# An attention and mixture-of-experts kernel: two more chunks through crossbar transposes, and another order of loads

## Chip, cores and metric

The kernel runs on one core of one Trainium2 chip. The metric is device time in microseconds (us) of one execution, the median of several executions. The profile comes from one execution of its own, and its span is the time from the first to the last instruction that it shows.

## What is computed

Two stages follow each other. The first is a linear attention with decay, for 4 batches, 8 heads, 768 time steps and 48 numbers per head. The second sends every one of the 3072 resulting rows (384 numbers each) through four experts, all of them, and adds their outputs with weights.

```python
# B, H, S, D = 4, 8, 768, 48
for t in range(S):
    cur = np.einsum('bhd,bhe->bhde', u[None] * kt, vt)
    y[:, :, t] = np.einsum('bhd,bhde->bhe', rt, state + cur)
    state = w[None, :, :, None] * state + np.einsum('bhd,bhe->bhde', kt, vt)
# x: (3072, 384), rows in the order batch, time
p = domain_probs / (domain_probs.sum(-1, keepdims=True) + 1e-09)
for e in range(4):
    h = np.maximum(x @ w1[e], 0.0)       # w1[e]: 384 x 1024
    out += p[:, e:e + 1] * (h @ w2[e])   # w2[e]: 1024 x 384
```

## The kernel before

**Tiling.** Time is cut into chunks of 128 steps. Chunk ci belongs to batch ci % 4 and time block ci // 4, so there are 24 chunks, and four chunks in a row (one of each batch) make a "sub-block" sc, six in all. All matrix work is in bf16, loads and accumulations in f32.

**Attention of a chunk.** R and K (r and k of the chunk) are scaled with powers of the decay on VectorE (DVE) or GpSimd (POOL), written into the buffer RK (line 332). RK is transposed for each pair of heads, which gives RKT. TensorE (PE) multiplies the two halves of RKT to scores (At, line 436), DVE multiplies those with a triangular mask (AtM, line 445), and PE multiplies by V and by the running state S (Y, lines 467 and 474). POOL forms r*k*u (ruk, lines 345 and 353), DVE sums it per head (dcoef, line 366), and POOL multiplies it by V (dv, line 371). Ysb is Y plus dv (line 483). The state is renewed through PE (line 515), DVE (line 530) and POOL (line 535). Ysb is transposed into xTe, the input of the experts.

**Two ways to transpose.** With `ci < DMAT` a chunk is transposed on PE against an identity matrix (RK at line 394, Ysb at line 500), and ScalarE (ACT) or DVE copies the result out of PSUM into RKT and xTe. With `ci >= DMAT` SP issues a crossbar DMA that transposes from SBUF to SBUF (RKT at line 378, xTe at line 490), and no engine copies. The same number decides over the scores: from DMAT on, an even chunk and the odd one after it are multiplied together in one job of PE ("paired"), which begins when both have their RKT. The odd chunk's scores then take a "tr" and an "mm" bank of PSUM in place of two "At" banks:

```python
dmat = ci >= DMAT
...
paired = ci >= DMAT
tags = ("tr", "mm") if paired and ci % 2 else ("At", "At")
```

**Experts.** A slot is one expert e on one sub-block sc. Its first layer (l1) fills hT_ps in eight groups: chunk by chunk, with 128 columns a matmul (line 596), in the slots (0,0), (0,1) and (1,1), and for the four chunks together, with 512 columns (line 602), in all others. ACT applies the ReLU (lines 611 and 613). The second layer (l2, line 632) is eight matmuls of 384 columns for each chunk, then DVE or ACT adds it into oacc with the weight of the expert (lines 640 and 642). The order of the slots is (0,0), (1,0), (0,1), (1,1), (2,0), (2,1), (3,0), (3,1), and then the four experts of each further sub-block.

**Weights.** w1 and w2 of an expert come in three pieces each (576, 576 and 384 KB) into eight staging tiles (wst) and are cast to bf16 into w_sb on ACT, DVE or POOL (lines 72, 74 and 76). A group of l1 needs only the pieces that hold its columns.

**What sets the order.** SP issues all loads, all crossbar transposes and all stores, in one queue. Its loads come in a written order, the string `ORDER` (line 219): K, R and V with a chunk number, "w1e0.1" for piece 1 of w1 of expert 0, "p" for the probabilities. From chunk 14 on the rest follows chunk by chunk. All other orders come from a planner that runs as the program is built (from line 675): every piece of work is a job with the engines it may run on, what it needs, a rank and the buffers it takes and gives back. The planner plays them through and writes down which engine takes which job when. The instructions are then issued per engine in that order, each engine strictly in line. So an instruction that has to wait holds up all that was planned behind it on its engine or queue. What an instruction really needs is enforced by semaphores whether or not the job lists it. In the first 20 us, where PE has too little work, matmuls on a constant (line 173) are put into its gaps.

Of the kernel before, what the change touches and what calls it, by code (L numbers as in the profile page):

```python
# [19 lines left out]
def kernel(  # L20
# [109 lines left out]

    WARM, NSPIN = 6.6, 6
    TAIL = {"T": 0.27, "V": 0.17, "A": 0.20, "P": 0.17, "S": 0.0}
    DMAT = 8
    BACKLOG = 6.0
    HURRY = 30.0
    PAD_PE, PAD = 1.0, 0.4
# [13 lines left out]
    def job(name, on, run, needs=(), rank=0.0, takes=(), drops=(), moves=None,  # L150
            behind=()):
        j = Job()
        j.behind = behind
        j.name, j.on, j.run, j.needs, j.rank = name, on, run, list(needs), rank
        j.takes, j.drops, j.moves = takes, drops, moves
        for k in drops:
            tokens[k] = tokens.get(k, 0) + 1
        j.pad = 0.0
        ci = name[1] if isinstance(name, tuple) and name[0] in ATT else -1
        if ci >= SUB:  # L160

            j.pad = PAD_PE if "T" in on else PAD
        j.no = len(jobs)
        assert name not in jobs
        jobs[name] = j
# [49 lines left out]
    def load_p():  # L215
        load_job("prow", (0.36, 2), lambda: nc.sync.dma_start(
            prow, moe_domain_probs.rearrange("(n p) e -> n p e", p=C)))

    ORDER = ("K1 R1 K0 R0 V0 R2 K2 V1 w1e0.1 w1e0.2 K3 w1e0.0 R3 V2 w2e0.0 V3 w2e0.1 w2e0.2 p w1e1.2 "
             "w1e1.1 R4 w1e1.0 K5 K4 w2e1.0 w2e1.2 w2e1.1 R5 V4 w1e2.2 w1e2.1 K6 w1e2.0 V5 K7 w2e2.2 "  # L220
             "w2e2.1 w2e2.0 R6 V6 K8 V7 R7 w1e3.2 w1e3.0 K9 w1e3.1 w2e3.0 V9 R9 R8 V8 V11 V10 R11 "
             "K10 R10 K12 K11 w2e3.1 V12 w2e3.2 R13 R12 K13 V13 " +
             " ".join(f"c{i}" for i in range(14, TOTC))).split()
    for what in ORDER:
        if what == "p":
# [87 lines left out]
    def attention(ci):  # L313
        b, c = ci % B, ci // B
        RK = RKB[ci % NRK]
        dmat = ci >= DMAT

        rk = float(ci)
        on_pe = -20.0 + 0.01 * ci
        pre = [("S", ci - NRK), ("T", ci - NRK, 1)] if ci >= NRK else []  # L320
        if ci >= 2 * SUB:

            e_g, sc_g, one = SLOTS[ci - LEAD - (ci % 2 if ci >= DMAT else 0)]
            pre.append(("l1", e_g, sc_g, 0, 0))
# [44 lines left out]
        def dv():  # L369
            tl["dv", ci] = work.tile([128, H, D], F32, tag="dv", bufs=3, name="dv")  # L370
            nc.gpsimd.tensor_mul(tl["dv", ci], tl["Vt", ci],  # L371
                                 tl["dcoef", ci].to_broadcast((128, H, D)))
        job(("dv", ci), {"P": 0.82}, dv, [("dcoef", ci)], rk - 0.4, (("dv", ci),), (("inp", ci),))

        if dmat:
            def tr():
# [47 lines left out]

        paired = ci >= DMAT
        tags = ("tr", "mm") if paired and ci % 2 else ("At", "At")
# [118 lines left out]
    for ci in range(TOTC):  # L545
        attention(ci)
# [309 lines left out]
```

## Time and profile before

| | |
|---|---|
| Median of 4 runs | 297.04 us (296.8 to 299.72) |
| Profiled execution | 297.05 us, its span 295.3 us |
| PE busy | 286.5 us, 97% of the span |
| DVE busy | 153.5 us, 52% |
| ACT busy | 153.0 us, 52% |
| POOL busy | 103.5 us, 35% |
| Granted clock of TensorE | 1.0 throughout |
| Moved by DMA | 37.66 MB, DMA engines full for about the first 90 us |

A busy share says how long an engine had an instruction in it. For PE the ends of the matmuls are modelled and neighbours overlap, so a single duration (326 ns for 384 columns) is longer than the time that it adds. What it adds is read from one start to the next. The chain of waits, followed back from the last instruction, is on PE for 81% of the span and on transfers for 7%. Here is its summary in the page, share of the span by engine and line:

```profile
PE 81%; DMA 7%; SPq 4%; POOL 2%; DVE 2%; issue 2%; ACT 2%; POOLq 0%; DVEq 0%
PE out_ps L632 37%; PE hT_ps L602 34%; DMA wst<-in_moe_w_dram 7%; PE hT_ps L596 4%; SPq L191 3%; PE At_ps L436 1%; PE Y_ps L474 1%; PE St_ps L515 1%; PE Y_ps L467 1%; POOL S L535 1%; ACT w_sb L72 1%; SPq L202 1%; POOL ruk L353 1%; DVE RK L332 1%; POOL dv L371 1%
```

### The profile page before, as it was taken

To read this page: it belongs to the slowest core of one execution; us is meant where nothing else is said; L and a number is where in the kernel's file an instruction comes from. 1 tells how busy PE (TensorE), PEld (TensorE's weight loads), DVE (VectorE), ACT (ScalarE), POOL (GpSimd) and SP (SyncE) were. 2 spreads that over 40 slices of the span, in tenths; PEclk is the share of its full clock that TensorE was granted. 3 is DMA by queue.
4 is the path that set the end of the run, shared out by engine and by line. 5 is a ranking of instruction groups with operands and counts; after the bars stand their busy time and mean duration, and the time that the engine had idled before them with its cause. 6 is when DMAs were issued, how large, how long until landed. Compare 5 with 4: busy or idle time off the path is not lost.

```text
span 295.3 us, 5781 instructions
## 1 busy us (share of the span) xinstructions
PE 286.5 (97%) x2264; PEld 169.3 (57%) x2293; DVE 153.5 (52%) x298; ACT 153.0 (52%) x251; POOL 103.5 (35%) x138
## 2 busy tenths in 40 slices
PE   8989999999989999999999999999999999999995
PEld 2777556868745555555555555555555555555553
DVE  6966879588494857526537436545404322101223
ACT  3685958754484444464543564443464444565440
POOL 3783243838949556443522443501000000000000
PEclk9999999999999999999999999999999999999999
DMA  7999999899999397392093393130340100200003
GB/s 147 270 259 338 258 275 300 192 300 188 242 179 178 72 201 193 95 196 47 16 175 82 109 175 61 28 71 29 97 83 0 27 2 27 80 2 0 0 2 107
DMA packets 111199, 37.66 MB, mean 128 GB/s; under 512 B 99242, under 2 KB 111148, under 8 KB 111172
## 3 DMA queue, kind: packets, MB, share of 16 engines
q1 hardware_dynamic: 111156, 37.29, 52.8%
q8 instruction: 18, 0.29, 0.4%
q14 instruction: 9, 0.07, 0.1%
q10 hardware_dynamic: 16, 0.00, 0.0%
HBM read 26.79 MB, written 4.72 MB: 107 GB/s over the span
## 4 chain that ended last, share of the span: by engine, by line
PE 81%; DMA 7%; SPq 4%; POOL 2%; DVE 2%; issue 2%; ACT 2%; POOLq 0%; DVEq 0%
PE out_ps L632 37%; PE hT_ps L602 34%; DMA wst<-in_moe_w_dram 7%; PE hT_ps L596 4%; SPq L191 3%; PE At_ps L436 1%; PE Y_ps L474 1%; PE St_ps L515 1%; PE Y_ps L467 1%; POOL S L535 1%; ACT w_sb L72 1%; SPq L202 1%; POOL ruk L353 1%; DVE RK L332 1%; POOL dv L371 1%
## 5 line engine op out<-in xcount | busy, mean ns | idle before, releaser
L613 ACT ACTIVATE hTs<-hT_ps 128x512 bf16<-128x512 f32 x168 | 99.5, 597 | 94.0 <-PE hT_ps L602 89.0
L632 PE MATMUL out_ps<-w_sb,hTs 128*128 128x384 bf16 x760 | 138.8, 326 | 0.3 <-DVE oacc L642 0.2
L602 PE MATMUL hT_ps<-xTe,w_sb 128*128 128x512 bf16 x475 | 122.0, 379 | 2.2 <-ACT hTs L613 0.8
L632 PEld LDWEIGHTS <-hTs 128*128 128x128 bf16 x760 | 72.6, 98 | 53.2 <-issue 0.5
L642 DVE SCALAR_TENSOR_TENSOR oacc<-out_ps,p_nat,oacc 128x384 f32<-128x384 f32 x71 | 43.7, 616 | 89.4 <-PE out_ps L632 89.2
L602 PEld LDWEIGHTS <-w_sb 128*128 128x128 bf16 x504 | 47.0, 98 | 47.6 <-issue 1.0
L445 DVE TENSOR_TENSOR AtM<-At_ps,mask 128x512 bf16<-128x512 f32 x48 | 30.8, 682 | 16.3 <-PE At_ps L436 16.3
L345 POOL TENSOR_TENSOR ruk<-Rt,Kt 128x384 f32<-128x384 f32 x24 | 24.9, 1040 | 40.9 <-DMA Kt<-in_k_dram 28.6
L371 POOL TENSOR_TENSOR dv<-Vt,dcoef 128x384 f32<-128x384 f32 x24 | 20.1, 840 | 44.1 <-DVE Ysb L483 30.0
L353 POOL TENSOR_TENSOR ruk<-ruk,U_sd 128x384 f32<-128x384 f32 x23 | 23.4, 1019 | 0.9
L640 ACT ACTIVATE oacc<-out_ps,p_nat 128x384 f32<-128x384 f32 x24 | 13.9, 582 | 14.3 <-PE out_ps L632 14.1
L72 ACT CAST w_sb<-wst 128x1152 bf16<-128x1152 f32 (+1 forms) x13 | 13.7, 1053 | 13.8 <-DMA wst<-in_moe_w_dram 13.5
L535 POOL TENSOR_TENSOR S<-Tn,wC 64x192 bf16<-64x192 f32 x32 | 18.6, 580 | 5.4 <-DVE Tn L530 4.0
L366 DVE TENSOR_REDUCE dcoef<-ruk 128x8 f32<-128x384 f32 x24 | 13.1, 547 | 13.9 <-POOL ruk L353 13.8
L596 PE MATMUL hT_ps<-xTe,w_sb 128*128 128x128 bf16 x288 | 18.6, 219 | 1.0 <-ACT w_sb L72 0.9
L596 PEld LDWEIGHTS <-w_sb 128*128 128x128 bf16 x288 | 16.8, 98 | 2.2 <-ACT w_sb L72 1.2
L611 ACT ACTIVATE hTs<-hT_ps 128x512 bf16<-128x512 f32 x24 | 14.3, 597 | 6.2 <-PE hT_ps L596 5.0
L332 DVE TENSOR_TENSOR RK<-Kt,W_sd 128x384 bf16<-128x384 f32 x20 | 15.8, 796 | 1.0 <-DMA Kt<-in_k_dram 0.9
L483 DVE TENSOR_TENSOR Ysb<-Y_ps,dv 128x384 bf16<-128x384 f32 x24 | 13.2, 552 | 5.0 <-PE Y_ps L474 4.9
L76 POOL CAST Vb<-Vt 128x384 bf16<-128x384 f32 x20 | 10.9, 546 | 9.0 <-PE St_ps L515 3.7
L530 DVE TENSOR_TENSOR Tn<-S,St_ps 64x192 f32<-64x192 bf16 x32 | 11.2, 349 | 2.7 <-PE St_ps L515 2.0
L332 DVE TENSOR_TENSOR RK<-Rt,W_sd 128x384 bf16<-128x384 f32 x20 | 12.0, 599 | 1.1 <-DMA Rt<-in_r_dram 0.9
(67 smaller groups left out, 134.4 us busy)
## 6 DMA issues: line engine op xcount, KB each, us to landing
wst<-in_moe_w_dram SPq DMA_DIRECT2D x16, 576.0 KB, 6.4
Kt<-in_k_dram SPq DMA_DIRECT2D x24, 192.0 KB, 3.9
Rt<-in_r_dram SPq DMA_DIRECT2D x24, 192.0 KB, 3.7
Vt<-in_v_dram SPq DMA_DIRECT2D x24, 192.0 KB, 3.6
out_dram<-oacc SPq DMA_DIRECT2D x23, 192.0 KB, 1.9
wst<-in_moe_w_dram SPq DMA_DIRECT2D x8, 384.0 KB, 6.5
RKT<-RK SPq DMA_TRANSPOSE x16, 3.2
xTe<-Ysb SPq DMA_TRANSPOSE x16, 2.4
```

The lines of the kernel that those rows point to most:

```text
L72: nc.scalar.copy(o, i)
L332: eng.tensor_mul(RK[:, i, :, 0:D], tl[("Kt", "Rt")[1 - i], ci], tl["W", i] if ci < SUB and i not in on_pool else W_sd[i])
L345: nc.gpsimd.tensor_mul(tl["ruk", ci], tl["Rt", ci], tl["Kt", ci])
L353: nc.gpsimd.tensor_mul(tl["ruk", ci], tl["ruk", ci], U_sd)
L371: nc.gpsimd.tensor_mul(tl["dv", ci], tl["Vt", ci], tl["dcoef", ci].to_broadcast((128, H, D)))
L445: nc.vector.tensor_mul(tl["AtM", ci][:, j], tl["At", ci, j], mask[:, None, :].to_broadcast((128, NP, C)))
L535: nc.gpsimd.tensor_mul(S_new[pr, :, cl], tl["Tn", ci][pr], wC[pr, :, None].to_broadcast((P2, NP, D)))
L596: nc.tensor.matmul(ps[:, i, :], w1_sb[:, e, db, (fb + i) * 128:(fb + i + 1) * 128], xTe[:, db, s0, :], start=(i == 0 and db == 0), stop=(i ...
L602: nc.tensor.matmul(ps[:, 0:n, :].rearrange("p a b -> p (a b)"), w1_sb[:, e, db, fb * 128:(fb + 1) * 128], xTe[:, db, s0:s0 + n, :].rearran ...
L613: nc.scalar.activation(hTs[:, fb, s0:s0 + n, :], ps[:, 0:n, :], AF.Relu)
L632: nc.tensor.matmul(ps, tl["hTs", e, sc][:, fb, s, :], w2_sb[:, e, fb, :], start=(fb == 0), stop=(fb == NFB - 1))
L642: nc.vector.scalar_tensor_tensor(tl["oacc", ci], in0=tl["o", e, ci], scalar=pe, in1=tl["oacc", ci], op0=ALU.mult, op1=ALU.add)
```

## The change

Three edits. DMAT goes from 8 to 6, so chunks 6 and 7 are transposed by DMAs, and their scores are computed as a pair. The order of the loads up to chunk 13 is another one, with the same 67 loads. And the job that forms dv lists the load of V among the things it needs, beside dcoef; the instruction itself is the same.

```diff
-    DMAT = 8
+    DMAT = 6
...
-    ORDER = ("K1 R1 K0 R0 V0 R2 K2 V1 w1e0.1 w1e0.2 K3 w1e0.0 R3 V2 w2e0.0 V3 w2e0.1 w2e0.2 p w1e1.2 "
-             "w1e1.1 R4 w1e1.0 K5 K4 w2e1.0 w2e1.2 w2e1.1 R5 V4 w1e2.2 w1e2.1 K6 w1e2.0 V5 K7 w2e2.2 "
-             "w2e2.1 w2e2.0 R6 V6 K8 V7 R7 w1e3.2 w1e3.0 K9 w1e3.1 w2e3.0 V9 R9 R8 V8 V11 V10 R11 "
-             "K10 R10 K12 K11 w2e3.1 V12 w2e3.2 R13 R12 K13 V13 " +
+    ORDER = ("V0 R1 K0 R0 K1 R2 w1e0.1 K2 V1 w1e0.2 w1e0.0 R3 V2 K3 w2e0.0 V3 w2e0.1 p w2e0.2 w1e1.2 "
+             "K5 R4 w1e1.0 K4 w1e1.1 w2e1.0 R5 w2e1.1 w2e1.2 w1e2.1 w1e2.0 V4 w1e2.2 V5 K7 K6 R7 R6 "
+             "w2e2.2 V7 V6 R8 w2e2.0 R9 w2e2.1 V8 w1e3.1 K8 K9 w1e3.2 w1e3.0 V9 K10 K11 R10 R11 V10 "
+             "R12 w2e3.1 V11 R13 K13 w2e3.0 V12 K12 w2e3.2 V13 " +
              " ".join(f"c{i}" for i in range(14, TOTC))).split()
...
-        job(("dv", ci), {"P": 0.82}, dv, [("dcoef", ci)], rk - 0.4, (("dv", ci),), (("inp", ci),))
+        job(("dv", ci), {"P": 0.82}, dv, [("dcoef", ci), ("Vt", ci)], rk - 0.4, (("dv", ci),), (("inp", ci),))
```

## The prediction

> **What bounds the kernel now.** I read the busy times by stretch first, then TensorE's waits, its timeline where the moved chunks lie, and last the transfers. In the rows below the columns are the stretch, its length, busy time of the engines with instruction counts, granted clock, busy share of the DMA engines, GB/s.
>
> ```profile
> 0.00:20.00 20.00, 17.09 (x196) 11.46 (x197) 14.62 (x42) 11.89 (x21) 12.39 (x22) 1.00 0.89 216
> 20.00:30.00 10.00, 9.88 (x139) 8.01 (x137) 6.39 (x17) 6.04 (x11) 4.81 (x5) 1.00 1.11 328
> ...
> 60.00:70.00 10.00, 9.87 (x111) 6.68 (x109) 9.93 (x19) 4.37 (x4) 4.78 (x7) 1.00 1.03 262
> 70.00:80.00 10.00, 10.00 (x137) 7.99 (x134) 4.58 (x10) 5.94 (x10) 9.37 (x14) 1.00 1.03 205
> 80.00:90.00 10.00, 9.14 (x72) 4.93 (x72) 8.32 (x16) 7.55 (x12) 6.29 (x8) 1.00 0.98 211
> 90.00:100.00 10.00, 9.72 (x75) 5.29 (x75) 6.86 (x13) 2.99 (x5) 7.79 (x11) 1.00 0.72 138
> ```
>
> TensorE (first busy column) is full from 20 us on: the stretches between 20 and 250 us together leave 2.55 us idle, 1.14 of it between 80 and 100. At the same time the DMA engines are full until 90 us. So two things run at their limit side by side, and PE sets the end as long as the loads keep it fed. Before 20 us much of PE's busy time is filler (matmuls of line 173); real work follows without a gap from 18.82 us, when the first expert's weights are there. TensorE's own waits confirm it:
>
> ```profile
> PE hT_ps L596 <- ACT w_sb L72: 0.9, 2, 0.5
> PE hT_ps L602 <- ACT hTs L613: 0.8, 1, 0.8
> ```
>
> They are us in total, times, longest. Hardly anything is there to recover by waiting less.
>
> **What the Trainium skill says.** "Trainium Kernel Development and Optimization", Performance Expectations, calls matmul busy time a poor measure, since matmuls overlap. I therefore checked spacing: eight matmuls of 384 columns take 1.30 us start to start in the chain, again and again up to 290 us, and other work leaves the gaps. PE is really full. "VectorE: DVE Perf Modes", The three transpose paths, prices a 128x128 transpose at 390 ns on TensorE and 1309 ns by crossbar DMA. The trace disagrees for runs of them: on PE eight take 0.45 us, 56 ns each; a DMA of eight tiles lands after 3.2 us, not 10.5. "Advanced Engine Details and Errata", X-Bar Transpose (TRN2), says such DMAs are as fast as regular ones; I use that below. "DMA: Bandwidth & Descriptors", Queues, rings and completion order, says that what SP issues shares one row of rings, consumed in order: a transpose stands behind the loads issued before it. The trace agrees: 4.7 us at most to landing, in the loaded stage, against 3.1 at least.
>
> **The change, part by part.**
>
> *1. Transposes and scores of chunks 6 and 7 (DMAT 8 to 6).* PE's timeline, columns start, duration, then what:
>
> ```profile
> 56.47 0.61 PE L394 MATMUL RKT_ps<-ident,RK 128*128 128x128 bf16 x8
> 56.92 1.46 PE L632 MATMUL out_ps<-w_sb,hTs 128*128 128x384 bf16 x8
> ...
> 60.28 0.40 PE L436 MATMUL At_ps<-RKT 64*128 64x128 bf16 x8
> 60.61 0.62 PE L394 MATMUL RKT_ps<-ident,RK 128*128 128x128 bf16 x8
> 61.07 2.76 PE L632 MATMUL out_ps<-w_sb,hTs 128*128 128x384 bf16 x16
> ...
> 72.13 0.33 PE L500 MATMUL xT_ps<-ident,Ysb 128*128 128x128 bf16 x3
> 72.30 1.46 PE L632 MATMUL out_ps<-w_sb,hTs 128*128 128x384 bf16 x8
> ...
> 77.68 0.62 PE L436 MATMUL At_ps<-RKT 64*128 64x128 bf16 x16
> 78.23 2.77 PE L632 MATMUL out_ps<-w_sb,hTs 128*128 128x384 bf16 x16
> ```
>
> Start to next start: each L394 group 0.45 and 0.46, each L500 group 0.17 (the other one is at 67.44, followed at 67.61). Scores alone cost 0.33 and 0.34 (60.28 and 64.33), a pair 0.55. PE sheds 0.45 + 0.46 + 2 x 0.17 + (0.67 - 0.55) = **1.37 us**, all in the full stage. ACT loses two copies of 1.01 us, DVE two of 0.36; neither is the bound, so I count nothing.
>
> In their place SP issues two transposes RKT<-RK and two xTe<-Ysb, about 1.24 and 1.18 us of SP each, in the stage where its queue carries all loads. The page's issues (KB each, median us to landing):
>
> ```profile
> wst<-in_moe_w_dram SPq DMA_DIRECT2D x16, 576.0 KB, 6.4
> ...
> RKT<-RK SPq DMA_TRANSPOSE x16, 3.2
> xTe<-Ysb SPq DMA_TRANSPOSE x16, 2.4
> ```
>
> What they take of the DMA engines has no row. From the stretches: 70 to 80 us, with two RKT transposes, moved 205 GB/s where 60 to 70, equally busy, moved 262; 10 us x 57/262 = 2.2 us, or 1.1 each. By the skill's "as fast as regular", estimated at 262 GB/s, RKT (256 KB) takes 1.0 and xTe (96 KB) 0.4. I take 2 x 1.1 + 2 x 0.4 = 3.0 us by which later loads slip; between 0 and 3.0 reaches the end, see 3. Chunk latency grows too: PE transpose plus copy was about 1.7 us (56.47 to 58.17), now 3.2 to 4.7; Xout 0.5 to 1 us, now 2.4 to 3.3. Chunk 6's scores also wait for chunk 7. Cover: R7 moves forward by 2304 KB in the order and R6 by 1344, some 9.8 and 5.7 us at 20.4 MB in 87 us (0.235 MB/us), far more than the added latency. Four masks of 0.65 us now come in one row on DVE, which is full from 60 to 70; the two pairs of scores hold one of four "mm" banks for about 2.6 us. I count 0, bound 0.5.
>
> *2. The start.* I added up the order. K0 and R0 keep their places, w1e0.1 lies 384 KB earlier, w1e0.0 192 KB earlier. The ACT row that opens PE's full stretch is
>
> ```profile
> 17.61 1.15 ACT L72 CAST w_sb<-wst 128x1152 bf16<-128x1152 f32 x1 [0.65 <-DMA wst<-in_moe_w_dram]
> ```
>
> 192 KB at 216 GB/s is 0.9 us. Chunk 1 has its xTe at 18.06 and chunk 2's V comes earlier too, so PE can fill up 0.9 us earlier. K3 comes 960 KB later, 4 us, but chunk 3's hidden layer was computed only at 28.4 us with its input there by 26. Yet w1e1.1 now comes 1152 KB later, about 33 us instead of 28.5, and ready after its cast at some 34.3. PE would by then have used up expert 0 and five of eight groups of expert 1. The lead survives in part: gain **0.4**, bounds 0 and 0.9.
>
> *3. The loads around 60 us.* w2e2.1 moves back 1728 KB. It was cast at about 52.2 to 52.9 and used from 61; 1728/235 = 7.4 us plus 2.2 for two RKT transposes ahead of it makes it ready at 62.5. What can PE do without it? From 36.6 us: second half of expert 1 (32 x 0.1625 = 5.2), first half of expert 2 (5.2), chunks 4 and 5 of experts 0 and 1 (4 x 2.65 = 10.6), their attention 3.0: until 60.6; scores, Y and state of chunks 6 and 7 (1.65): until 62.2 if their transposes land by 57. The hole is 0 to 2 us; I take **+0.6**. Later loads (w1e3 576 KB later, w2e3 576 KB) have cover: the first half of expert 2 on chunks 4 to 7 alone is 5.2 us, and the chunks they compete with come sooner. Of the 0.86 us idle at 80 to 90, which is ACT casting w2e3 pieces ahead of a ReLU, I take away 0.2; bounds -1.1 and +0.5.
>
> *4. dv needs Vt.* No instruction is added; the data dependence existed already. POOL waited 8.9 us for Vt in front of two dv (39.88 and 46.72), with the next chunk's ruk queued behind; now other POOL work can stand there. PE did not wait for it, so I count 0: POOL idles 65% of the span, and that is the cover. Bounds 0 and, if ruk in front makes a dv late by its 1.0 us, 0.5.
>
> Sum: -1.37 - 0.4 + 0.6 - 0.2 + 0 = **-1.4**, span 295.3 to 293.9. Profiled execution 297.05 = 295.3 + 1.75 around it, and the median of the runs 297.04 is the same. Forecast 295.6.
>
> **Rivals.** *A, nothing gained:* the loads are the clock of the stage to 90 us, and 3.0 us of added DMA time reaches PE in part or in full. With half of it, 297.0 - 1.37 + 1.5 = 297.2; in full, 298.7. I give 297.9. For it: DMA share 1.03 at 60 to 80. Against: PE idles only 0.13 us from 50 to 80, so some lead exists.
>
> *B, slower by a blocked queue:* SP issues in order. If it reaches a transpose before DVE has written RK or Ysb, every load behind it waits. The queue holds a lead of about 4 us (576 KB land after 6.4 us and need 2.2 themselves). SP waited 5.7 us for RK and 11.1 for Ysb at worst in the run before, harmless because the loads were already out. Such waits at 50 to 65 us cost 1.7 to 7 beyond the lead, and PE has no slack there: -1.4 + 5 = 300.6 (299 to 303). It decides from an SP wait of about 7 us, the lead plus 3. Against: R6, R7, K6, K7 stand together in the new order, so RK is early.
>
> *C, everything holds:* -1.37 - 0.9 - 1.1 = 293.7. That requires no hole at 34 or 62 us.
>
> That the edit doesn't do what it says is excluded: the choice is made by chunk number, with no data condition.
>
> **Numbers.** Forecast (294.1 to 297.0) 0.50, A 0.20, B 0.19, C 0.11. A measurement of this kernel tells about 1% from no change, that is 294.07 and 300.01. Faster is C with 0.11; slower is B with 0.19; the rest, forecast and A, is 0.70. The range 293.5 to 300.2 leaves out half of B and the edge of C, about 0.15.
>
> **What would show it.** Right: 48 transposing matmuls of L394 in place of 64, 18 of L500 in place of 24, and 18 transposes of each kind on SP; PE busy lower by 1.4; the first L602 no later than 30.2; no PE wait on w_sb over 1 us. Wrong: a hole of PE at 33 to 35 or 59 to 64 ending in a cast of w_sb (A), or an SP wait over 7 us before L378 or L490 between 48 and 66 followed by a drop in the DMA share (B).

## The result, and the profile after

| | before | after |
|---|---|---|
| Median on the same chip | 297.92 us (64 runs) | 299.64 us (43 runs) |
| Ratio of the runs, 95% interval | | 1.0044 [1.0029, 1.0060] |
| Profiled execution, its span | 297.05 us, 295.3 us | 296.98 us, 295.2 us |
| PE busy | 286.5 us | 284.2 us |
| PE idle from 20 to 100 us | 1.55 us | 2.24 us |
| PE idle from 100 to 120 us | 0.16 us | 1.48 us |
| Carried by SP's queue | 37.29 MB | 38.01 MB |

The changed kernel is slower by 0.44%, that is 1.3 us: 297.04 x 1.0044 = 298.35 us, where 295.6 was forecast. (The ratio leaves out runs over 1.5% above the fastest of their kernel; the medians of the table are of all runs and lie 0.6% apart.) The time lies within the stated range, but on the other side of the kernel before. One warning for reading what follows: single executions of one kernel scatter by about 1%, and the profiled one of after, 296.98 us, is the fastest of its 43 (296.98 to 301.68). Its profile, no longer than the one of before, shows where the kernel is tight, not the loss; the ratios carry that.

Busy time by stretch of the kernel after, columns as in the prediction (start and end, length, PE, PEld, DVE, ACT, POOL, clock, DMA share, GB/s):

```profile
20.00:30.00 10.00, 9.21 (x114) 7.25 (x116) 6.77 (x19) 7.76 (x12) 3.12 (x4) 1.00 1.03 285
60.00:70.00 10.00, 9.87 (x75) 5.65 (x76) 9.91 (x16) 3.82 (x6) 5.24 (x6) 1.00 0.94 235
70.00:80.00 10.00, 9.73 (x139) 7.64 (x140) 5.25 (x12) 6.86 (x12) 5.78 (x9) 1.00 0.84 159
80.00:90.00 10.00, 9.95 (x78) 5.86 (x78) 7.30 (x12) 5.17 (x10) 7.94 (x10) 1.00 1.11 240
90.00:100.00 10.00, 9.06 (x66) 4.96 (x64) 9.27 (x16) 3.22 (x6) 8.62 (x9) 1.00 1.06 213
```

Later stretches, with PE alone (start and end, length, PE busy, clock, DMA share, GB/s). The first row is the kernel before, the other two are the kernel after:

```profile
100.00:120.00 20.00, 19.84 (x155) 1.00 0.69 160
...
100.00:110.00 10.00, 9.89 (x92) 1.00 1.02 180
110.00:120.00 10.00, 8.62 (x75) 1.00 0.66 161
```

Read the last two columns. Before, the DMA engines came free at 90 us (share 0.72 from 90 to 100); now they are busy until 110. From 70 to 80 us only 159 GB/s are moved, where 205 were. There the new transposes of Ysb of chunks 6 and 7 run close to two of RK (chunks 8 and 9) that the kernel before had too. The engines are not busy all the time even there (share 0.84): from 74 to 76 us next to nothing moves (60 and 19 GB/s in the two microseconds), though the queue holds work. Why stays open. So "DMA time" below means time of the queue, whether bytes flow in it or not.

PE has lost 0.67 us between 20 and 30, 0.66 between 90 and 100 and most, 1.27, between 110 and 120. Its waits (us in total, times, longest):

```profile
PE hT_ps L602 <- DMA xTe<-Ysb: 1.3, 1, 1.3
PE RKT_ps L394 <- POOL RK L332: 1.3, 2, 0.7
PE out_ps L632 <- ACT hTs L613: 0.9, 1, 0.9
```

The first stands at 113.46 us, the third at 93.33, and one of the second at 20.39. None of them ends in a cast of w_sb. PE's timeline at chunks 6 and 7 (start, duration, then what):

```profile
59.36 0.62 PE L436 MATMUL At_ps<-RKT 64*128 64x128 bf16 x16
59.91 5.37 PE L632 MATMUL out_ps<-w_sb,hTs 128*128 128x384 bf16 x32
```

The pair of scores runs at 59.36 and nothing waits there. SP issues without a pause, in its timeline from 63 to 79 us:

```profile
64.25 4.05 SPq L191 DMA_DIRECT2D Kt<-in_k_dram  x2
68.39 1.35 SPq L490 DMA_TRANSPOSE xTe<-Ysb  x1
69.82 2.64 SPq L378 DMA_TRANSPOSE RKT<-RK  x2
72.56 1.21 SPq L490 DMA_TRANSPOSE xTe<-Ysb  x1
...
77.46 1.00 SPq L205 DMA_DIRECT2D wst<-in_moe_w_dram  x1
```

Ysb of chunk 6 is ready at about 67.0 us, but two K loads hold SP for 4.05 us in front. Why an issue takes so long isn't settled: the view of SP's waits lays 2.7 us of the second K load to POOL (ruk), whose input buffers the loads refill, but the queue ahead that has to move on would look alike. The load that closes the fence is w2e3.1, the first piece of w2 of expert 3 to be issued; its place in time is a clock of the queue that I use below.

The page's issues (KB, median us to landing) and its line of SP's queue (packets, MB, share of 16 engines' span):

```profile
q1 hardware_dynamic: 114100, 38.01, 55.6%
...
wst<-in_moe_w_dram SPq DMA_DIRECT2D x16, 576.0 KB, 5.4
...
RKT<-RK SPq DMA_TRANSPOSE x18, 3.9
xTe<-Ysb SPq DMA_TRANSPOSE x18, 3.0
```

The packets of the queue took 55.6% of 295.2 = 164.1 us, before 52.8% of 295.3 = 155.9. That is 8.2 us more for 0.72 MB more. (Shares above 1.00 in the rows above show that packets overlap, so this isn't moving time alone.)

### The profile page after: what moved, and what is told of

It reads as the page before. It is cut to its first block, busy times and chain, and to the rows that moved or that the text cites. A ratio compares the mean times of both kernels' runs of the same rounds, so it can differ in the third digit from the quotient of the medians.

```text
span 295.2 us, 5722 instructions
## 1 busy us (share of the span) xinstructions
PE 284.2 (96%) x2233; PEld 167.4 (57%) x2259; DVE 155.7 (53%) x298; ACT 150.8 (51%) x250; POOL 102.1 (35%) x135
## 3 DMA queue, kind: packets, MB, share of 16 engines
q1 hardware_dynamic: 114100, 38.01, 55.6%
## 4 chain that ended last, share of the span: by engine, by line
PE 83%; DMA 6%; SPq 4%; DVE 4%; issue 2%; POOL 1%; ACT 0%; DVEq 0%; POOLq 0%
PE out_ps L632 39%; PE hT_ps L602 33%; PE hT_ps L596 4%; SPq L191 2%; DMA Vt<-in_v_dram 2%; PE At_ps L436 2%; DMA RKT<-RK 2%; DMA wst<-in_moe_w_dram 1%; DMA xTe<-Ysb 1%; SPq L202 1%; PE Y_ps L474 1%; PE St_ps L515 1%; PE Y_ps L467 1%; DVE oacc L642 1%; DVE AtM L445 1%
## 5 line engine op out<-in xcount | busy, mean ns | idle before, releaser
L602 PE MATMUL hT_ps<-xTe,w_sb 128*128 128x512 bf16 x478 | 120.7, 379 | 2.9 <-DMA xTe<-Ysb 1.3
L602 PEld LDWEIGHTS <-w_sb 128*128 128x128 bf16 x504 | 47.2, 98 | 49.0 <-issue 1.4
L353 POOL TENSOR_TENSOR ruk<-ruk,U_sd 128x384 f32<-128x384 f32 x23 | 24.8, 1083 | 1.1
L72 ACT CAST w_sb<-wst 128x768 bf16<-128x768 f32 (+1 forms) x15 | 14.7, 978 | 8.9 <-DMA wst<-in_moe_w_dram 8.8
L535 POOL TENSOR_TENSOR S<-Tn,wC 64x192 bf16<-64x192 f32 x32 | 18.0, 564 | 3.0 <-DVE Tn L530 1.6
L332 DVE TENSOR_TENSOR RK<-Rt,W_sd 128x384 bf16<-128x384 f32 x20 | 13.3, 669 | 3.1 <-DMA Rt<-in_r_dram 2.9
L332 DVE TENSOR_TENSOR RK<-Kt,W_sd 128x384 bf16<-128x384 f32 x20 | 14.4, 722 | 0.0
L74 DVE CAST w_sb<-wst 128x1152 bf16<-128x1152 f32 x9 | 10.1, 1121 | 4.1 <-DMA wst<-in_moe_w_dram 4.1
```

The costliest lines, as they stand in the source:

```text
L72: nc.scalar.copy(o, i)
L332: eng.tensor_mul(RK[:, i, :, 0:D], tl[("Kt", "Rt")[1 - i], ci], tl["W", i] if ci < SUB and i not in on_pool else W_sd[i])
L353: nc.gpsimd.tensor_mul(tl["ruk", ci], tl["ruk", ci], U_sd)
L535: nc.gpsimd.tensor_mul(S_new[pr, :, cl], tl["Tn", ci][pr], wC[pr, :, None].to_broadcast((P2, NP, D)))
L602: nc.tensor.matmul(ps[:, 0:n, :].rearrange("p a b -> p (a b)"), w1_sb[:, e, db, fb * 128:(fb + 1) * 128], xTe[:, db, s0:s0 + n, :].rearran ...
```

## The experiments

Ratios are to the kernel before on the same chip, with the 95% interval. "Order" is the new order of loads together with the dv edit, which belongs to it. A, B and C are the rivals of the prediction.

**Which edit does it?** First the changed kernel once more, and its parts alone.

> The changed kernel once more, for a second profile and as the yardstick of the three parts beside it. Both theories expect 0.3 to 0.6% above the kernel before (about +1.3 us), with holes of TensorE of 1 to 4 us in total between 85 and 120 us that the first profile (2.3 us there) may show smaller or larger.

Measured 1.0039 [1.0017, 1.0061]. The loss is there again. Its profile has PE busy for only 8.39 of the 10 us from 70 to 80, in PE's windows (stretch, length, PE busy, clock, DMA share, GB/s):

```profile
70.00:80.00 10.00, 8.39 (x114) 1.00 0.98 165
```

and there PE waits 0.69 us for hTs (at 70.94) and 0.92 for RKT (at 77.33), from a crossbar transpose that the kernel before had too, and that now stands behind a new one in the queue. The hole at 113 us is not there. So the same program pays in other places from one execution to the next.

Transposes and pairs alone, in the old order:

```diff
-    DMAT = 8
+    DMAT = 6
```

> DMAT = 6 with the old order of loads and the old needs of dv. Theory T (transposes): chunks 6 and 7 get their xTe later through the DMA than through TensorE, the slots that use them move back, and chunks 10 and 11, which are held until one of those slots begins, come late for the third sub-block: slower than before by 1 us or more, with a hole of TensorE near 100 to 115 us. Theory O (order of loads): the transposes alone save their 1.4 us of TensorE work: 0.5 to 1.4 us faster than before, no hole over 0.5 us after 95 us.

Measured 1.0124 [1.0080, 1.0168], 3.7 us slower, as theory T has it, but with the hole at 70 to 82 us and not near 100 to 115. PE's windows:

```profile
70.00:80.00 10.00, 5.58 (x76) 1.00 1.08 166
80.00:90.00 10.00, 8.97 (x117) 0.83 1.01 241
```

and the timeline shows where the 4.4 us between 70 and 80 went, for instance

```profile
76.31 0.34 PE L515 MATMUL St_ps<-Vb,RK 128*128 128x96 bf16 x4 [1.46 <-DVE Tn L530]
...
81.03 0.88 PE L596 MATMUL hT_ps<-xTe,w_sb 128*128 128x128 bf16 x12 [2.02 <-DMA xTe<-Ysb]
```

A transpose issued at 54.87 landed at 63.0, 8.1 us later. So the new order removes most of a loss that the first edit brings by itself. About half of that loss is a lower clock of TensorE (last section).

Order alone (after with DMAT = 8), and the dv edit alone:

```diff
-    DMAT = 6
+    DMAT = 8
```

> The new order of loads and the new need of dv, with DMAT = 8, so that chunks 6 and 7 stay on TensorE. Theory O: slower than before by 1.3 us or more, with TensorE waiting for weights of expert 3 (w2e3.0 lies 3072 KB further back) near 93 us. Theory T: same as before within 0.6 us or faster, no wait for xTe near 113 us.

> The new order and the need of dv alone once more, as the yardstick for the two kernels built on it: 0.4% faster to 0.1% slower than before, as in its first run.

> Only the need of dv for the load of V is added. Both theories: same as before within 0.6 us (0.2%). If it is over 0.6 us slower or faster, the replanned order of GpSimd is a cause of its own.

Measured 0.9985 [0.9956, 1.0014] and 0.9998 [0.9977, 1.0018] for the order, 1.0021 [0.9991, 1.0052] for dv. The order is worth nothing that can be measured. So the loss stands between order alone and order with DMAT = 6.

**Which transposes?** In the changed kernel each kind is given back to TensorE by itself, then the pairing.

In e5 TensorE transposes Ysb of chunks 6 and 7 (line 489):

```diff
-        if dmat:
+        if ci >= 8:
```

> The changed kernel, but the xTe of chunks 6 and 7 are transposed on TensorE again (RKT stays with the DMA, scores stay paired). Theory X (the second crossbar step: Ysb waits 2 us for SP behind loads and then 4 us for its landing, which starves TensorE between 70 and 82 us): the loss goes, 0.3% faster to 0.1% slower than before, no wait of TensorE for xTe before 82 us. Theory R (the first crossbar step, RKT, and the DMA time it takes from the loads): stays 0.3 to 0.6% slower than before.

In e6 TensorE transposes RK, the scores are unpaired, and xTe alone comes by DMA:

```diff
-        dmat = ci >= DMAT
+        dmat = ci >= 8
...
-        paired = ci >= DMAT
+        paired = ci >= 8
...
-        if dmat:
+        if ci >= 6:
```

> The other half: RKT of chunks 6 and 7 and their single scores on TensorE as before the change, only their xTe by DMA, new order of loads. Theory X: 0.3 to 0.8% slower than before. Theory R: as fast as the new order alone, 0.4% faster to 0.1% slower than before.

In e7 only the pairing goes:

```diff
-        paired = ci >= DMAT
+        paired = ci >= 8
```

> The changed kernel with the scores of chunks 6 and 7 computed singly, each as soon as its RKT is there. Theory P (pairing makes chunk 6 wait for chunk 7 and takes a bank that the experts need): the loss shrinks to 0.2% or less. Theories X and R: as the changed kernel, 0.3 to 0.7% slower than before, as TensorE has 0.12 us more to do.

Measured 1.0010 [0.9989, 1.0031], 0.9982 [0.9963, 1.0001] and 1.0032 [1.0011, 1.0054]. With one kind alone, the saving on PE included, no loss against the kernel before is shown; the two together cost 0.4%; and nothing of it is seen to come from the pairing. Neither theory X nor theory R foretold both e5 and e6. It looks less like one bad transfer than like a sum that exceeds what the stage can spare, though the interval of e5 reaches to that of the changed kernel.

**Which wait?** Four edits are each aimed at one visible hole.

In e8 chunks 10 and 11 may start at an earlier slot, against the hole at 113 us:

```diff
-            e_g, sc_g, one = SLOTS[ci - LEAD - (ci % 2 if ci >= DMAT else 0)]
+            e_g, sc_g, one = SLOTS[4 if ci in (10, 11) else ci - LEAD - (ci % 2 if ci >= DMAT else 0)]
```

> The changed kernel with chunks 10 and 11 tied to the beginning of slot (2,0) in place of (2,1), which begins late now. Theory G (the late slot holds these two chunks back, and the third sub-block begins with a hole near 113 us): that hole goes and the time falls to before or below it. Theories X and R: the holes at 70 to 82 us stay, 0.2 to 0.5% slower than before.

In e11 the inputs of chunks 6 and 7 are loaded earlier:

```diff
-             "K5 R4 w1e1.0 K4 w1e1.1 w2e1.0 R5 w2e1.1 w2e1.2 w1e2.1 w1e2.0 V4 w1e2.2 V5 K7 K6 R7 R6 "
-             "w2e2.2 V7 V6 R8 w2e2.0 R9 w2e2.1 V8 w1e3.1 K8 K9 w1e3.2 w1e3.0 V9 K10 K11 R10 R11 V10 "
+             "K5 R4 w1e1.0 K4 w1e1.1 w2e1.0 R5 w2e1.1 w2e1.2 w1e2.1 w1e2.0 V4 K7 K6 R7 R6 w1e2.2 V5 "
+             "V7 V6 w2e2.2 R8 w2e2.0 R9 w2e2.1 V8 w1e3.1 K8 K9 w1e3.2 w1e3.0 V9 K10 K11 R10 R11 V10 "
```

> The changed kernel with K7 K6 R7 R6 moved ahead of w1e2.2 and V5 (576 KB, 2.5 us earlier) and V7 V6 ahead of w2e2.2. Theory L: the xTe of chunk 7 comes 1.5 to 2.5 us earlier (74 to 75 us) and half of the loss goes, 0 to 0.25% slower than before, if w1e2.2 is still in time for the group at 48 us. Theory D: 0.3 to 0.6% slower than before as the DMA time is the same.

In e15 (on e6) and e16 (on order alone) K3 is loaded earlier, against the wait at 20 us:

```diff
-    ORDER = ("V0 R1 K0 R0 K1 R2 w1e0.1 K2 V1 w1e0.2 w1e0.0 R3 V2 K3 w2e0.0 V3 w2e0.1 p w2e0.2 w1e1.2 "
+    ORDER = ("V0 R1 K0 R0 K1 R2 w1e0.1 K2 V1 w1e0.2 w1e0.0 K3 V2 R3 w2e0.0 V3 w2e0.1 p w2e0.2 w1e1.2 "
```

> A version meant to be faster than both: new order of loads with K3 and R3 exchanged, need of dv, RKT of chunks 6 and 7 on TensorE, their xTe by DMA (as e6). TensorE's wait of 1.04 us for chunk 3 near 20 us, which every kernel with the new order shows, should shrink to 0.3 us or less: 0.25 to 0.5% faster than before. If that lead is lost again at the next weights, 0.1 to 0.3% faster, as e6.

> The new order with K3 and R3 exchanged and the need of dv, nothing by DMA before chunk 8 (as e12): 0.15 to 0.4% faster than before if the wait near 20 us reaches the end, 0.1% slower to 0.15% faster if it doesn't.

Measured 1.0026 [1.0006, 1.0047], 1.0061 [1.0031, 1.0091], 1.0060 [1.0035, 1.0084] and 1.0003 [0.9982, 1.0024]. In e8 the hole at 113 us went and holes of 1.16, 0.60 and 1.28 us stood at 70.5, 76.6 and 95.7 instead. In e11 those at 70 to 82 went (0.20 us is left at 70.43), and one of its new ones reads

```profile
PE hT_ps L596 <- DVE xTe L74: 1.0, 1, 1.0
```

at 50.5 us. In e15, which I took for an improvement of e6, the wait at 20 us only changed its name (Y_ps for Vb, 0.75 us), and the kernel came out 0.8% slower than e6: a miss. Holes move and the loss does not go, as in a stage limited by a resource and not by one late transfer. There is a limit to this method: every edit makes the planner lay out the work anew. e15 and e6 lie 0.8% apart, with no cause that I can name, which is more than the 0.44% in question. So a single pair of kernels proves little here, and only e17 and e18 below keep all orders.

**Lateness or DMA time?** A moved transpose makes its chunk later and also takes DMA time. Four kernels on the base of order alone (TensorE transposes) separate the two. e9 adds two transposes of RK and two of Ysb of chunks 6 and 7, which nobody reads (to make room for them, three small constants share other buffers):

```diff
+        if ci in (6, 7):
+            def extra_t():
+                t = work.tile([128, 2, NP, C], BF16, tag="xRKT", bufs=2, name="xRKT")
+                nc.sync.dma_start_transpose(t.rearrange("p i q c -> p (i q) c"),
+                                            RK.rearrange("p i h d -> p (i h d)"))
...
+            def extra_x():
+                t = work.tile([128, NDB, 128], BF16, tag="xxTe", bufs=1, name="xxTe")
+                nc.sync.dma_start_transpose(t, tl["Ysb", ci])
```

> New order of loads and need of dv, chunks 6 and 7 transposed on TensorE as before the change, and beside that the four crossbar transposes of the changed kernel once more into tiles that nobody reads: their DMA time and their place in SP's queue without their latency. Theory D (the 3 us of DMA time, or SP's time, push the later loads back): 0.3 to 0.6% slower than before, as the changed kernel. Theory L (what counts is when chunk 7's xTe is there): as the new order alone, 0.4% faster to 0.1% slower than before, with the xTe of chunk 7 by 73.5 us.

e10 lets the planner set TensorE's transposes of Ysb of these chunks 4 us later, e13 8 us:

```diff
+        if name in (("X", 6), ("X", 7)):
+            j.pad = 4.0
```

> New order of loads and need of dv, chunks 6 and 7 on TensorE, no extra DMA, but the planner puts the transposes of their Ysb 4 us later: the latency without the DMAs. Theory L: the xTe of chunk 7 comes at 75 to 77 us in place of 72 and the kernel is 0.2 to 0.5% slower than before. Theory D: 0.4% faster to 0.1% slower than before.

> As e10, with the transposes of chunks 6 and 7's Ysb planned 8 us later in place of 4, no extra DMA. If lateness of these two xTe costs time (theory L), a doubled dose brings them to about 76 us, as in the changed kernel, and the kernel is 0.4 to 0.8% slower than before. If the 0.24% of e10 was chance, it stays between 0 and 0.3%.

e14 joins e9 and e13:

> e13 and e9 together: the four extra crossbar transposes that nobody reads, and the late xTe, all real work of chunks 6 and 7 still on TensorE. If DMA time and lateness are two causes, they add: 0.2 to 0.3% above e13, 0.6 to 1.0% slower than before, which is the changed kernel's loss plus the 0.46% (1.37 us) of TensorE work that it saves. If only lateness counts: as e13 within 0.1%.

Measured 1.0024 [1.0005, 1.0043], 1.0024 [1.0001, 1.0048], 0.9976 [0.9950, 1.0003] and 1.0082 [1.0052, 1.0111]. No cost of lateness alone is seen: with xTe of chunk 7 at 78.0 us, later than in the kernel after (76.1), e13 is no slower than before. e10, at 72.4 us, came out 0.24% slower, as theory L had it; but more lateness would then cost more, and e13 is faster. e14 lies within its forecast and yet misses its reason: it is 1.06% above e13, not 0.2 to 0.3. PE's windows of e13:

```profile
70.00:80.00 10.00, 10.00 (x126) 1.00 0.93 218
80.00:90.00 10.00, 10.00 (x97) 1.00 0.58 141
```

and of e14:

```profile
70.00:80.00 10.00, 8.87 (x104) 1.00 1.04 166
80.00:90.00 10.00, 9.01 (x103) 1.00 0.96 234
```

xTe of chunk 7 is equally late in both (78.0 and 78.2 us). The edit adds four transfers whose result is not used, and the planner lays out the rest anew. In e13 the DMA engines are idle 0.4 of the time from 80 to 90 us and PE is full from 30 to 250 us; in e14 they are busy to 100 and PE loses 2.1 us in these 20, and 0.45 in the next 10. One of its waits, at 71.42, is

```profile
PE hT_ps L619 <- ACT w_sb L72: 1.1, 1, 1.1
```

which is a weight that came late (its lines are numbered differently, L619 is L602 of the changed kernel). From e13 to e14 is 1.06% or 3.1 us; from order alone to e9 it was only 0.3 to 0.4%, 1 us. SP's queue gives the delay without PE: w2e3.1 is issued in order alone (e12) at

```profile
72.74 0.57 SPq L205 DMA_DIRECT2D wst<-in_moe_w_dram  x1
```

and in e9 at

```profile
76.26 0.70 SPq L205 DMA_DIRECT2D wst<-in_moe_w_dram  x1
```

3.5 us later, for 704 KB. All kernels with the new order and its loads whole agree: the five without the four transposes (e3, e10, e12, e13, e16) issue it at 71.3 to 74.2 us, the seven with them (after, e1, e7, e8, e9, e11, e14) at 76.3 to 78.3, on average 4.9 us later; with the two of Ysb alone (e6) it is 74.6, with the two of RK alone (e5) 76.1. All seven are slower than before with an interval above 1; of the five only e10 is. Chance in the planner's layout is an unlikely reason for that division, as nearly every one of these kernels has a layout of its own.

**Give the DMA time back, keep everything else.** The strictest test holds the order of every engine's instructions fixed. Two pieces of w1 of expert 3 load one third of their rows, 768 KB less, and the cast repeats that third; so two thirds of the rows of these pieces are left out of expert 3's first layer. (ROWS is 1 for these two pieces and 3 for all others.) At the 0.235 MB/us of the prediction this frees 3.3 us of the queue. e17 does it in the kernel after, e18 in the kernel before.

```diff
-                nc.sync.dma_start(t[:, 0:(bb - a) * Dm].rearrange("p (d f) -> p d f", d=NDB),
-                                  w1_v[e][:, :, a * 128:bb * 128])
+                nc.sync.dma_start(t[:, 0:(bb - a) * Dm].rearrange("p (d f) -> p d f", d=NDB)[:, 0:ROWS(e, i)],
+                                  w1_v[e][:, 0:ROWS(e, i), a * 128:bb * 128])
```

> The changed kernel with every instruction of every engine in the same order, but two loads made smaller: of w1e3.1 and w1e3.0 only the first 128 of 384 rows are loaded and used three times over (768 KB less, 3.3 us at 0.235 MB/us, between 56 and 66 us), so this part of expert 3's first layer is left out. Theory D (the crossbar transposes' 3 us of DMA time delay the loads behind them, and those delays reach TensorE): giving the DMA time back makes it 0.2 to 0.6% faster than before, as the 1.37 us of TensorE work saved remains. If DMA time isn't the cause: 0.2 to 0.5% slower than before, as the changed kernel.

> The same two loads made smaller in the kernel before, all orders as they were: the control, same part left out. Theory D with a stage that has some slack in the kernel before: same to 0.25% faster, clearly less than the changed kernel gains. If any kernel here gains 0.5% or more from 768 KB less, the load stage bounds the kernel before as well.

Measured 0.9923 [0.9899, 0.9948] and 0.9954 [0.9930, 0.9977], both more than was expected. PE's windows of e17:

```profile
60.00:70.00 10.00, 9.95 (x77) 1.00 0.81 182
70.00:80.00 10.00, 10.00 (x144) 1.00 0.91 196
90.00:100.00 10.00, 9.00 (x64) 1.00 1.07 179
```

From 60 to 80 PE now has no gap to speak of; those at 92 and 112 us are still there. The kernel before gains 0.46% (1.4 us) from 768 KB less; the kernel after falls from 1.0044 to 0.9923, 1.2% or 3.6 us. So the loads set part of the end already before the change, and clearly more of it after: the two gains differ by 0.75%, about twice the half-width of that difference's interval (0.37, put together from those of the ratios). What a microsecond of the queue is worth can't be read from this pair, as w2e3.1 is issued only 1.9 us earlier in the profile of e17 than in that of after, and 3.5 us earlier in e18 than in before. With the DMA time given back on both sides, after against before is 0.9923 / 0.9954 = 0.997: TensorE's saving of the transposes can show then, though 0.3% is within the intervals.

None of these runs parts the time that the transposes take of the DMA engines from the time that SP spends on issuing them, 1.2 us at least for each; either can delay the loads behind.

No version that does the whole work is shown to beat the kernel before. e6 and e13 lie lowest, and their intervals just touch 1.

## Why the prediction was wrong

*What bounds the kernel.* I saw two resources at their limit side by side and then argued with one. "PE idles only 0.13 us from 50 to 80" was taken as a sign of lead. It is none: e18 shows that the loads set part of the end before the change, 1.4 us for 768 KB, with PE as full as that.

*Part 1, the step that failed.* The savings on PE are what was said: 48 transposing matmuls of L394 and 18 of L500, a pair in 0.55 us (59.36 to 59.91). The step that failed is the term for the DMA time, "between 0 and 3.0 reaches the end". It went into the sum only through one hole at w2e2.1, +0.6 in part 3, and was then taken for covered. The runs show 1 us at the end from the four transposes in e9, 3.1 us from e13 to e14, and 1.3 + 1.37 = 2.7 us in the change itself, if order is 0 and PE's saving is real.

Its size was also low: the loads behind the transposes came 4.9 us later on average, not 3.0. The mean packet time of SP's queue is 158.2 us over seven profiles of kernels without these four transposes (before, e3, e4, e10, e12, e13, e16) and 165.0 over eight with them (after, e1, e2, e7, e8, e9, e11, e14), 6.9 more with a standard error of 1.1; 4.2 in each of the pairs e12/e9 and e13/e14. The sizes of the packets in the traces tell whose time it is. A transpose has packets of 256 bytes here (1024 for RKT, 384 for xTe), and these alone account for 4.8 of the 6.9 us.

Two readings made the term small. The 205 GB/s of 70 to 80 us already contain the 512 KB of the two transposes in it, so the 2.2 us drawn from that row are what they cost beyond their bytes at 262 GB/s, not the whole. And 262 GB/s was the rate of a mixed stretch. By their own packet time in the kernel after, transposes moved 179 GB/s, the loads of r, k and v (packets of 192 bytes) 192 GB/s, and packets of 1536 bytes, which are weights and stores, 335 GB/s. So "as fast as regular ones", from the Trainium skill, "Advanced Engine Details and Errata", X-Bar Transpose (TRN2), comes near here against the loads of r, k and v, and not against the weights.

*Part 1, latency.* "I count 0, bound 0.5" is not contradicted. e13 shows no cost of a late xTe, and the pair at 59.36 did not wait; a late RKT by itself was not tried. The cover in the order was there, but it covered the delay of these chunks and not the delay of the loads behind the transposes.

*Part 2, the start.* PE's full stretch begins at 17.46 instead of 18.82 us, 1.36 us earlier, and the first L602 at 30.01, within the 30.2 asked for. But chunk 3's slack was no slack: PE is in line, and its transposes wait in front of other work:

```profile
20.39 0.40 PE L394 MATMUL RKT_ps<-ident,RK 128*128 128x128 bf16 x4 [0.69 <-POOL RK L332]
...
21.30 0.40 PE L436 MATMUL At_ps<-RKT 64*128 64x128 bf16 x8 [0.35 <-DVE RKT L74]
```

1.36 - 0.69 - 0.35 leaves 0.3, near the 0.4 counted, but by luck: these waits were not in the account, and of the lead only 0.18 us is left at the first L602 (30.01 against 30.19). w1e1.1, the one I feared, came in time.

*Part 3, loads around 60 us.* The hole at w2e2.1 did not come; PE's waits have none on a weight over 0.2 us. The holes came later and spread: at 93 and 113 us in the kernel after, on hTs and xTe, and at 70 to 80 us in e1, on hTs and RKT. Adding up what work PE has in stock until one named weight arrives was the wrong account, because the planner moves the stock with every edit.

*Part 4, dv.* 0 was counted, and 1.0021 [0.9991, 1.0052] does not contradict it.

*Rivals.* A came true in its mechanism and its number (297.2 to 298.7; 298.35 results), though not with the mark that I gave for it, a wait on a cast of w_sb at 59 to 64: the kernel after shows none over 0.2 us, and e8 and e14 show one of 1.2 and 1.1 us, at 70.5 and 71.4. I gave A too little because I compared PE's idle time, where I should have compared what a stage's DMA time is worth. B is refuted: from 48 to 82 us SP never waited for a transpose's data by more than 1.45 us (at 49.57, before a transpose of RK). C needed the loads to be free.

## What to carry to other kernels

When one engine is busy to 99% and the DMA engines to 100% in the same stage, both can bound it, and a small idle time of the engine is no sign that the loads have slack. Before work is moved from an engine to DMA there, price it in time of the queue, at the rate that such transfers show in the trace, and count more than nothing of it: here 1 to 3 us of some 5 reached the end. Look for a stage where the queue has gaps. The cheapest test is to take bytes away from a load and leave all orders alone: it tells whether the loads set the end.

## What the hardware showed that I had not expected

SP's issue time is not a constant. The issue of one load took from 0.4 us to 4.82 (a K load of the kernel before, at 48.29), that of one transpose from 1.2 to 3.2 (e2, at 59.79). All that stands behind a long issue is issued later. Whether a long one waits for room in the queue or for a buffer stays open; no semaphore that it waits for came during the one of 3.62 us at 22.00 in the kernel after, so a buffer isn't the reason for all of them.

In e2 the granted clock of TensorE fell after the idle stretch, in PE's windows of two microseconds:

```profile
80.00:82.00 2.00, 0.97 (x16) 0.93 0.88 176
82.00:84.00 2.00, 2.00 (x28) 0.50 1.05 243
84.00:86.00 2.00, 2.00 (x13) 0.72 1.10 319
86.00:88.00 2.00, 2.00 (x40) 1.00 1.16 298
```

PE was never idle for more than 2.02 us at once, but for 4.4 of the 10 us from 70 to 80. The Trainium skill, "TensorE: Matmul & The Clock Gate", Part 1: The HAM clock gate, has half clock after an idle window of about 3.4 us and full clock after a busy one. The 0.50 agrees, and so does its length: the four windows add up to 3.4 us at half clock. In this trace gaps of 2.02 us at most, close together, were enough. Starving PE thus cost more than the gaps: 3.4 us at half clock are 1.7 us of work lost, by estimate. It was no chance of the profiled execution, for all six runs of e2 have a mean clock of 0.993 or 0.994.
